# SwiGLU feed-forward on one core: the first 256 rows of x by a crossbar copy instead of TensorE transposes

## The chip, the core and the metric

The kernel runs on one core of a Trainium2 chip. The engines are TensorE (PE in the profile, its weight loads PEld), VectorE (DVE), ScalarE (ACT), GpSimd (POOL) and SyncE (SP). SP and ACT also issue the DMAs, each on a queue of its own; the profile calls these rows SPq and ACTq. The metric is the device time of one execution in microseconds (us), lower is better.

## The reference

x is 1 x 2048 x 640, w_gate and w_up are 640 x 1536, w_down is 1536 x 640, all bf16.

```
def reference(x, w_gate, w_up, w_down):
    g = silu(x @ w_gate)
    u = x @ w_up
    return (g * u) @ w_down
```

## The kernel before

TensorE multiplies over the partition axis, 128 at a time, so x is needed with its 640 columns on partitions: `xT`, 128 partitions x 5 blocks (`KD`) x 2048 rows. The weights lie in on-chip memory as `wg_sb`, `wu_sb` (5 blocks x 1536 columns) and `wd_sb` (12 blocks x 640 columns).

The 2048 rows are taken in four blocks (`sb`) of 512. In each block, for each of 12 column groups (`fc`) of 128, five matmuls of 512 columns make the gate projection `pg` and five the up projection `pu` in PSUM (line 193). ACT takes silu of `pg` into `sg` (line 214), DVE multiplies it by `pu` into `aT` (line 215). When the 12 groups are done, 12 matmuls with `wd_sb` as weights (line 261) make the last 128 output columns, and 4 x 12 matmuls (line 291) the first 512. The last four rows of x go another way: DVE computes their projections as row dot products (line 147) beside TensorE's work. The end of the program cuts the last rows' output into narrow pieces.

The first block begins in another order, in `head()`. TensorE first runs `N_WARM` = 18 matmuls on a tile of ones (`warm`, line 176), which wait only for DVE's memset of that tile (line 109). The first 256 rows of x then arrive as two plain loads of 128 rows (`x_sb`, line 86), one on SP and one on ACT. TensorE transposes them against an identity matrix, which GpSimd makes: five transposes of 128 x 128 for each of the two (`transpose_chunk`, line 185), two into one PSUM tile and three into another. ACT and DVE copy them to `xT` (line 190).

The gate projections of the first four column groups (`EARLY` = 4) follow, held in four PSUM tiles at once. They go block by block over `KD` and in halves of the 512 rows: first rows 0 to 255 for all five blocks, then rows 256 to 511. For block 0 the first half is cut again, into 128 rows and 128 rows. Thus 44 matmuls: 8 of 128 columns and 36 of 256. The four up projections come behind them, 20 matmuls of 512 columns, and from there the regular order.

The weights of the early gate projections, `wg_sb` columns 0 to 511, come as five loads of 128 KB, one for each `kd` (line 115), on SP except for `kd` = 1 on ACT. Behind them, SP's queue holds, in program order: the crossbar copy of x rows 256 to 511 (`turn_x`, line 105; a DMA that transposes on its way), the up weights of groups 0 and 1 and of groups 2 and 3 (line 83), the gate and up weights of groups 4 to 7 and of groups 8 to 11, `wd_sb`, the crossbar copy of rows 512 to 1023, and the loads for the four last rows. ACT, behind its two loads, loads its activation table and runs one silu on a column of ones (line 119), so that the table is there.

`keep_order` writes the issue order of TensorE, ACT, DVE and SP out by hand as the program has it. Waits are placed by the framework from the data that an instruction uses.

Of the kernel before, what the change touches and what calls it, by code (L numbers as in the profile page):

```python
# [7 lines left out]


@with_exitstack  # L10
def _body(
# [8 lines left out]
    nc = tc.nc  # L20
    P = nc.NUM_PARTITIONS
    f32 = mybir.dt.float32
    bf16 = mybir.dt.bfloat16
    ACT = mybir.ActivationFunctionType
    ALU = mybir.AluOpType

    B, S0, D = x.shape
    F = w_gate.shape[1]
    S = B * S0
    x2 = x.rearrange("b s d -> (b s) d")  # L30
    out2 = out.rearrange("b s d -> (b s) d")

    KD = D // P
# [4 lines left out]
    HALF = S_BLK // 2  # L38
    DA = 512
    Q = 32  # L40
    N_WARM = 18
    T = 4
    WT_STEP = 4
    ROW_J = 0
    EARLY = 4
# [3 lines left out]
    consts = ctx.enter_context(tc.tile_pool(name="consts", bufs=1))  # L49
    work = ctx.enter_context(tc.tile_pool(name="work", bufs=3))  # L50
    outp = ctx.enter_context(tc.tile_pool(name="outp", bufs=3))
    psum = ctx.enter_context(
        tc.tile_pool(name="psum", bufs=2, space=bass.MemoryType.PSUM)
    )

    ident = consts.tile([P, P], bf16)
    x_sb = consts.tile([P, HALF // P, D], bf16)
    xT = consts.tile([P, KD, S], bf16)
    wg_sb = consts.tile([P, KD, F], bf16)
    wu_sb = consts.tile([P, KD, F], bf16)  # L60
# [7 lines left out]
    row_s = consts.tile([P, KF, T], f32)  # L68
    prod = consts.tile([P, D], f32)

    make_identity(nc, ident[:])

    x_v = x2.rearrange("(c p) d -> p c d", p=P)
    xt_v = x2.rearrange("s (kd p) -> s kd p", p=P)
    wg_v = w_gate.rearrange("(kd p) f -> p kd f", p=P)
    wu_v = w_up.rearrange("(kd p) f -> p kd f", p=P)
# [2 lines left out]
    def wslice(a, b):  # L79
        return slice(a * P, b * P)  # L80

    def load_w(eng, dst, src, a, b):
        eng.dma_start(out=dst[:, :, wslice(a, b)], in_=src[:, :, wslice(a, b)])

    def load_x(eng, c0, c1):
        eng.dma_start(out=x_sb[:, c0:c1, :], in_=x_v[:, c0:c1, :])  # L86

    def issue_order(a, b):
        tc.add_manual_dep(
# [8 lines left out]
    def keep_order(engine):  # L98

        traced = [i for i in nc.cur_bb.bb.instructions if i.engine == engine]  # L100
        for a, b in zip(traced, traced[1:]):
            issue_order(a, b)

    def turn_x(r0, r1):
        nc.sync.dma_start_transpose(out=xT[:, :, r0:r1], in_=xt_v[r0:r1])

    ones = consts.tile([P, P], bf16)
    silu_first = consts.tile([P, 1], f32)
    nc.vector.memset(ones[:], 1.0)  # L109

    load_x(nc.sync, 0, 1)
    load_x(nc.scalar, 1, 2)
    for kd in range(KD):
        eng = nc.scalar if kd == 1 else nc.sync
        eng.dma_start(
            out=wg_sb[:, kd, wslice(0, EARLY)], in_=wg_v[:, kd, wslice(0, EARLY)]
        )
    turn_x(HALF, S_BLK)
    nc.scalar.activation(silu_first[:], ones[:, 0:1], ACT.Silu)  # L119
    for a in range(0, EARLY, 2):  # L120
        load_w(nc.sync, wu_sb, wu_v, a, a + 2)
    for a, b in W_CHUNKS:
# [6 lines left out]
    def turn_w(dst, src, f0, f1):  # L129
# [7 lines left out]
        out=x_row[:],  # L137
        in_=x2[S - T : S, :].rearrange("t d -> (t d)").partition_broadcast(P),
# [35 lines left out]
    def warm(n):  # L174
        for _ in range(n):
            nc.tensor.matmul(  # L176
                pw[:, 0:P], lhsT=ones[:], rhs=ones[:], start=True, stop=True
            )

    def transpose_chunk(c, parts):  # L180
        c_sl = slice(c * P, (c + 1) * P)
        for copy, tag, k0, k1 in parts:
            pt = psum.tile([P, k1 - k0, P], bf16, tag=tag, name="pt")
            for kd in range(k0, k1):
                nc.tensor.transpose(  # L185
                    out=pt[:, kd - k0, :],
                    in_=x_sb[:, c, kd * P : (kd + 1) * P],
                    identity=ident[:],
                )
            copy(out=xT[:, k0:k1, c_sl], in_=pt[:])  # L190

    def proj_step(ps, w_sb, fc, sb, c0, c1, kd):
        nc.tensor.matmul(  # L193
            ps[:, c0:c1],
            lhsT=w_sb[:, kd, fc * P : (fc + 1) * P],
            rhs=xT[:, kd, sb * S_BLK + c0 : sb * S_BLK + c1],
            start=(kd == 0 and c0 in (0, HALF)),
            stop=(kd == KD - 1),
        )

    def proj(ps, w_sb, fc, sb, c0, c1):
        for kd in range(KD):
            proj_step(ps, w_sb, fc, sb, c0, c1, kd)
# [6 lines left out]
    def gate(pg, pu, sb, fc, n_s):  # L210

        s0 = sb * S_BLK
        sg = work.tile([P, S_BLK], f32, name="sg")
        nc.scalar.activation(sg[:, 0:n_s], pg[:, 0:n_s], ACT.Silu)  # L214
        nc.vector.tensor_tensor(  # L215
            out=aT[:, fc, s0 : s0 + n_s], in0=sg[:, 0:n_s], in1=pu[:, 0:n_s], op=ALU.mult
        )

    def head():
        dve, act = nc.vector.tensor_copy, nc.scalar.copy  # L220
        split = [(act, "po_a", 0, 2), (dve, "po_b", 2, KD)]
        pgs = [
            psum.tile([P, S_BLK], f32, tag="gu", name="pg", bufs=4)
            for _ in range(EARLY)
        ]
        warm(N_WARM)
        for c in range(HALF // P):
            transpose_chunk(c, split)

        steps = [(0, 0, P), (0, P, HALF)]  # L230
        steps += [(kd, 0, HALF) for kd in range(1, KD)]
        steps += [(kd, HALF, S_BLK) for kd in range(KD)]
        for kd, c0, c1 in steps:
            for fc in range(EARLY):
                proj_step(pgs[fc], wg_sb, fc, 0, c0, c1, kd)

        for fc in range(EARLY):
            pu = psum.tile([P, S_BLK], f32, tag=("po_a", "po_b")[fc % 2], name="pu")
            proj(pu, wu_sb, fc, 0, 0, S_BLK)
            gate(pgs[fc], pu, 0, fc, S_BLK)  # L240
        keep_order(mybir.EngineType.PE)
        keep_order(mybir.EngineType.Activation)

    head()
    for sb in range(NSB):
        n_s = S_BLK if sb < NSB - 1 else S_BLK - T
# [26 lines left out]
        for q in range(P // Q):  # L273
            nc.scalar.dma_start(
                out=out2[
                    sb * S_BLK : sb * S_BLK + n_t, DA + q * Q : DA + (q + 1) * Q
                ].rearrange("(i r) c -> r i c", r=Q),
                in_=ot_q[q * Q : (q + 1) * Q, :].rearrange("r (i c) -> r i c", c=Q),
            )

        for j in range(SUB):
# [6 lines left out]
            for c0, c1, tag in cols:  # L288
# [14 lines left out]
                eng = nc.sync if c1 < D else nc.scalar  # L303
# [82 lines left out]
def kernel(tc, *args):  # L386
    _body(tc, *args)
    tc.close()
    tc.compile()
    _trim(tc.nc)  # L390
# [30 lines left out]
```

## Time and profile before

| | |
|---|---|
| median of 3 runs | 163.57 us |
| lowest and highest | 163.18, 163.78 us |
| span of the profiled execution, first to last instruction | 161.8 us |
| TensorE busy in the span | 159.4 us (99%), 808 matmuls |
| VectorE, ScalarE busy | 111.0 us (69%), 42.6 us (26%) |
| first gate matmul, first up matmul | 3.71, 8.79 us |
| moved by DMA | 15.86 MB |

The device time of the profiled execution itself is not recorded beside its span; the median of the runs is 1.8 us above the span. Times in the profile count from the first instruction of the span. A row of the timeline has its start, its length, the engine, the line in the kernel, the operation with output and inputs, and how many instructions are merged in it; in brackets stands how long the engine was idle ahead of it and what ended that. A matmul's length is longer than the distance to the next one, because matmuls are pipelined: the pace is read from the distances of the starts. A stretch row has the stretch, its length, the busy time of PE, PEld, DVE, ACT and POOL with their instructions, the granted clock of TensorE, the share of time in which the DMA engines were busy, and GB/s.

### The profile page before, as it was taken

The numbers are of one execution on the slowest core, as the hardware profiler recorded it, in microseconds if no ns is written. First come the engines' busy times: TensorE is split into PE (matmuls) and PEld (weight loads), VectorE is DVE, ScalarE is ACT, GpSimd is POOL, SyncE is SP. The second block draws the span as 40 slices with busy tenths as digits, with TensorE's granted clock in tenths as the row PEclk, the third lists the DMA queues.
The fourth block names the chain that finished last, engine by engine and source line by source line (L and its number), as shares of the span: only waits on it lengthen the run. The fifth ranks groups of instructions, "written<-read, shape, count | busy, mean of one in ns | idle before, by whom it ended". The sixth has DMA issues, their size and how long they took to land.

```text
span 161.8 us, 2142 instructions
## 1 busy us (share of the span) xinstructions
PE 159.4 (99%) x808; PEld 77.6 (48%) x808; DVE 111.0 (69%) x250; ACT 42.6 (26%) x74; POOL 0.6 (0%) x6
## 2 busy tenths in 40 slices
PE   8999999999999999999999999999999999999995
PEld 7854444444444444444444444444444444445454
DVE  2034223599569999989919999979964999993001
ACT  5051222112222222211222322221214222222121
POOL 1000000000000000000000000000000000000000
PEclk9999999999999999999999999999999999999999
DMA  6999999934189999003110000000321000000312
GB/s 212 231 351 349 361 248 231 222 75 91 34 192 159 235 236 184 4 0 34 65 65 0 0 4 2 0 0 3 62 67 34 0 0 0 0 0 4 48 41 73
DMA packets 41961, 15.86 MB, mean 98 GB/s; under 512 B 33504, under 2 KB 41824, under 8 KB 41952
## 3 DMA queue, kind: packets, MB, share of 16 engines
q1 hardware_dynamic: 33584, 14.93, 37.0%
q10 hardware_dynamic: 8368, 0.80, 3.5%
q8 instruction: 6, 0.10, 0.3%
q14 instruction: 3, 0.02, 0.1%
HBM read 6.88 MB, written 2.62 MB: 59 GB/s over the span
## 4 chain that ended last, share of the span: by engine, by line
PE 97%; DMA 2%; SPq 0%; DVE 0%; issue 0%
PE pg L193 32%; PE pu L193 32%; PE po_a L291 26%; PE po_t L261 6%; DMA wg_sb<-in_w_gate_dram 2%; SPq L86 0%; DVE ot_b L302 0%
## 5 line engine op out<-in xcount | busy, mean ns | idle before, releaser
L193 PE MATMUL pg<-xT,wg_sb 128*128 128x512 bf16 (+3 forms) x264 | 59.8, 363 | 0.1
L193 PE MATMUL pu<-xT,wu_sb 128*128 128x512 bf16 (+1 forms) x240 | 59.1, 379 | 0.0
L215 DVE TENSOR_TENSOR aT<-sg,pu 128x512 bf16<-128x512 f32 (+1 forms) x48 | 32.7, 682 | 32.3 <-PE pu L193 32.3
L214 ACT ACTIVATE sg<-pg 128x512 f32<-128x512 f32 (+1 forms) x48 | 28.4, 597 | 71.2 <-PE pg L193 67.4
L291 PE MATMUL po_a<-wd_sb,aT 128*128 128x512 bf16 (+4 forms) x228 | 42.8, 348 | 0.0
L147 DVE SCALAR_TENSOR_TENSOR prod<-wgT,x_row 128x640 f32<-128x640 bf16 x48 | 39.4, 821 | 1.5 <-DMA wgT<-in_w_gate_dram 0.4
L147 DVE SCALAR_TENSOR_TENSOR prod<-wuT,x_row 128x640 f32<-128x640 bf16 x48 | 39.4, 821 | 1.0
L193 PEld LDWEIGHTS <-wg_sb 128*128 128x128 bf16 x264 | 25.9, 100 | 26.8 <-DMA wg_sb<-in_w_gate_dram 0.4
L193 PEld LDWEIGHTS <-wu_sb 128*128 128x128 bf16 x240 | 23.4, 98 | 28.1 <-DMA wu_sb<-in_w_up_dram 0.3
L291 PEld LDWEIGHTS <-aT 128*128 128x128 bf16 x228 | 20.8, 98 | 21.7
L300 ACT CAST ot<-po_a 128x512 bf16<-128x512 f32 (+2 forms) x17 | 9.5, 559 | 31.8 <-PE po_a L291 20.2
L261 PE MATMUL po_t<-aT,wd_sb 128*128 128x512 bf16 (+1 forms) x48 | 10.4, 366 | 0.0
L261 PEld LDWEIGHTS <-wd_sb 128*128 128x128 bf16 x48 | 4.7, 98 | 5.1
L302 DVE CAST ot_b<-po_a 128x96 bf16<-128x96 f32 (+1 forms) x2 | 0.5, 240 | 9.7 <-PE po_a L291 9.6
L270 ACT CAST ot_t<-po_t 128x512 bf16<-128x512 f32 (+1 forms) x4 | 2.2, 559 | 11.6 <-PE po_t L261 11.6
L147 DVE DVE_READ_ACCUMULATOR prod<-wgT,x_row 128x1 f32 x48 | 3.9, 82 | 0.0
L147 DVE DVE_READ_ACCUMULATOR prod<-wuT,x_row 128x1 f32 x48 | 3.9, 82 | 0.0
L272 DVE STREAM_TRANSPOSE ot_q<-ot_t 128x512 bf16<-128x512 bf16 (+1 forms) x4 | 2.7, 676 | 1.7 <-ACT ot_t L270 1.7
L190 DVE COPY xT<-pt 128x384 bf16<-128x384 bf16 x2 | 0.7, 358 | 2.9 <-PE pt L185 2.9
L176 PE MATMUL pw<-ones 128*128 128x128 bf16 x18 | 2.1, 313 | 0.4 <-DVE ones L109 0.4
L176 PEld LDWEIGHTS <-ones 128*128 128x128 bf16 x18 | 1.8, 147 | 0.4 <-DVE ones L109 0.4
L119 ACT ACT_TABLE_LOAD x1 | 1.3, 1283 | 1.0 <-issue 1.0
(13 smaller groups left out, 4.7 us busy)
## 6 DMA issues: line engine op xcount, KB each, us to landing
wd_sb<-in_w_down_dram SPq DMA_DIRECT2D x1, 1920.0 KB, 13.0
out_dram<-ot SPq DMA_DIRECT2D x15, 128.0 KB, 1.7
wg_sb<-in_w_gate_dram SPq DMA_DIRECT2D x2, 640.0 KB, 7.9
wu_sb<-in_w_up_dram SPq DMA_DIRECT2D x2, 640.0 KB, 8.6
wu_sb<-in_w_up_dram SPq DMA_DIRECT2D x2, 320.0 KB, 4.7
x_row<-in_x_dram SPq DMA_DIRECT2D x1, 640.0 KB, 5.1
wg_sb<-in_w_gate_dram SPq DMA_DIRECT2D x4, 128.0 KB, 3.4
out_dram<-ot_q ACTq DMA_DIRECT2D x12, 32.0 KB, 1.9
```

The lines of the kernel that those rows point to most:

```text
L119: nc.scalar.activation(silu_first[:], ones[:, 0:1], ACT.Silu)
L147: nc.vector.scalar_tensor_tensor(out=prod[:], in0=wT[:, fc, :], scalar=1.0, in1=x_row[:, t, :], op0=ALU.mult, op1=ALU.mult, accum_out=acc[ ...
L176: nc.tensor.matmul(pw[:, 0:P], lhsT=ones[:], rhs=ones[:], start=True, stop=True)
L190: copy(out=xT[:, k0:k1, c_sl], in_=pt[:])
L193: nc.tensor.matmul(ps[:, c0:c1], lhsT=w_sb[:, kd, fc * P : (fc + 1) * P], rhs=xT[:, kd, sb * S_BLK + c0 : sb * S_BLK + c1], start=(kd == 0 ...
L214: nc.scalar.activation(sg[:, 0:n_s], pg[:, 0:n_s], ACT.Silu)
L215: nc.vector.tensor_tensor(out=aT[:, fc, s0 : s0 + n_s], in0=sg[:, 0:n_s], in1=pu[:, 0:n_s], op=ALU.mult)
L261: nc.tensor.matmul(po_t[:], lhsT=wd_sb[:, kf, DA:D], rhs=aT[:, kf, sb * S_BLK : sb * S_BLK + n_t], start=(kf == 0), stop=(kf == KF - 1),)
L270: nc.scalar.copy(ot_t[:], po_t[:])
L272: nc.vector.transpose(out=ot_q[:], in_=ot_t[:])
L291: nc.tensor.matmul(po[:], lhsT=aT[:, kf, s0 : s0 + P], rhs=wd_sb[:, kf, c0:c1], start=(kf == 0), stop=(kf == KF - 1),)
L300: nc.scalar.copy(ot[:], po[:])
```

## The change

The identity, `x_sb`, the two plain loads, the transposes on TensorE and the copies out of PSUM are taken out. Rows 0 to 255 of x come by one crossbar copy straight into `xT`, the first DMA on SP's queue. The first activation (with its table load) now stands ahead of ACT's two loads. Those two are the gate slices of `kd` 0 and 1; slices 2, 3 and 4 come as one load of 384 KB on SP, behind the crossbar copy. The second crossbar copy and all later loads follow in the order they had. The warm-up has 26 matmuls instead of 18. The first half of block 0 is no longer cut in two, so the early gate phase has 40 matmuls of 256 columns. TensorE has 802 matmuls and transposes in all, instead of 808.

```
-    N_WARM = 18
+    N_WARM = 26
...
-    ident = consts.tile([P, P], bf16)
-    x_sb = consts.tile([P, HALF // P, D], bf16)
...
-    make_identity(nc, ident[:])
...
-    load_x(nc.sync, 0, 1)
-    load_x(nc.scalar, 1, 2)
-    for kd in range(KD):
-        eng = nc.scalar if kd == 1 else nc.sync
+    def load_d(eng, k0, k1):
         eng.dma_start(
-            out=wg_sb[:, kd, wslice(0, EARLY)], in_=wg_v[:, kd, wslice(0, EARLY)]
-        )
+            out=wg_sb[:, k0:k1, wslice(0, EARLY)], in_=wg_v[:, k0:k1, wslice(0, EARLY)]
+        )
+
+    turn_x(0, HALF)
+    nc.scalar.activation(silu_first[:], ones[:, 0:1], ACT.Silu)
+    load_d(nc.scalar, 0, 1)
+    load_d(nc.scalar, 1, 2)
+    load_d(nc.sync, 2, KD)
     turn_x(HALF, S_BLK)
-    nc.scalar.activation(silu_first[:], ones[:, 0:1], ACT.Silu)
     for a in range(0, EARLY, 2):
         load_w(nc.sync, wu_sb, wu_v, a, a + 2)
...
-    def transpose_chunk(c, parts):
-        c_sl = slice(c * P, (c + 1) * P)
-        for copy, tag, k0, k1 in parts:
-            pt = psum.tile([P, k1 - k0, P], bf16, tag=tag, name="pt")
-            for kd in range(k0, k1):
-                nc.tensor.transpose(
-                    out=pt[:, kd - k0, :],
-                    in_=x_sb[:, c, kd * P : (kd + 1) * P],
-                    identity=ident[:],
-                )
-            copy(out=xT[:, k0:k1, c_sl], in_=pt[:])
...
         warm(N_WARM)
-        for c in range(HALF // P):
-            transpose_chunk(c, split)
-
-        steps = [(0, 0, P), (0, P, HALF)]
-        steps += [(kd, 0, HALF) for kd in range(1, KD)]
+        steps = [(kd, 0, HALF) for kd in range(KD)]
         steps += [(kd, HALF, S_BLK) for kd in range(KD)]
```

More of the change, by code (lines that the diff above doesn't have):

```diff
@@ L6 @@
 from concourse._compat import with_exitstack
-from concourse.masks import make_identity
 @with_exitstack
@@ L69, in _body @@
     prod = consts.tile([P, D], f32)
-    make_identity(nc, ident[:])
-    x_v = x2.rearrange("(c p) d -> p c d", p=P)
     xt_v = x2.rearrange("s (kd p) -> s kd p", p=P)
@@ L83, in load_w @@
         eng.dma_start(out=dst[:, :, wslice(a, b)], in_=src[:, :, wslice(a, b)])
-    def load_x(eng, c0, c1):
-        eng.dma_start(out=x_sb[:, c0:c1, :], in_=x_v[:, c0:c1, :])
     def issue_order(a, b):
@@ L219, in head @@
     def head():
-        dve, act = nc.vector.tensor_copy, nc.scalar.copy
-        split = [(act, "po_a", 0, 2), (dve, "po_b", 2, KD)]
         pgs = [
```

## The prediction

> **What bounds the kernel now.** I read the page first: engines' busy shares, then the chain that ended last.
>
> ```profile
> span 161.8 us, 2142 instructions
> ...
> PE 159.4 (99%) x808; PEld 77.6 (48%) x808; DVE 111.0 (69%) x250; ACT 42.6 (26%) x74; POOL 0.6 (0%) x6
> ...
> PE 97%; DMA 2%; SPq 0%; DVE 0%; issue 0%
> ```
>
> TensorE is busy 99% of the span, and the chain is TensorE but for 2% of DMA. The change touches only the head, so the next view is the chain in order of time.
>
> ```profile
> 0.45 3.21 DMA wg_sb<-in_w_gate_dram
> 3.71 5.21 PE pg L193 x44
> 8.92 4.37 PE pu L193 x20
> ...
> 148.85 11.10 PE po_a L291 x84
> ```
>
> A gate slice is issued at 0.45 and lands at 3.66; from 3.71 TensorE runs to the end. What happens before the first up matmul is therefore worth its own length, and everything behind it (20 up matmuls, then the rest) is unchanged. I compare one number: when the first up matmul starts. The timeline of the first 15 us gives it, and what stands in front of it.
>
> ```profile
> 0.00 0.39 SPq L86 DMA_DIRECT2D x_sb<-in_x_dram  x1
> 0.13 0.38 ACTq L86 DMA_DIRECT2D x_sb<-in_x_dram  x1
> ...
> 0.39 2.10 PE L176 MATMUL pw<-ones 128*128 128x128 bf16 x18 [0.39 <-DVE ones L109]
> 0.45 1.84 SPq L115 DMA_DIRECT2D wg_sb<-in_w_gate_dram  x4
> 0.54 0.45 ACTq L115 DMA_DIRECT2D wg_sb<-in_w_gate_dram  x1
> ...
> 1.02 1.28 ACT L119 ACT_TABLE_LOAD   x1 [1.02 <-issue]
> 2.31 1.25 PE L185 MATMUL pt<-ident,x_sb 128*128 128x128 bf16 x10
> 2.32 0.20 ACT L119 ACTIVATE silu_first<-ones 128x1 f32<-128x1 bf16 x1
> 2.33 1.91 SPq L105 DMA_TRANSPOSE xT<-in_x_dram  x1
> ...
> 3.60 0.36 DVE L190 COPY xT<-pt 128x384 bf16<-128x384 bf16 x1 [0.17 <-PE pt L185]
> 3.71 4.93 PEld L193 LDWEIGHTS <-wg_sb 128*128 128x128 bf16 x44 [0.41 <-DMA wg_sb<-in_w_gate_dram]
> 3.71 5.21 PE L193 MATMUL pg<-xT,wg_sb 128*128 128x128 bf16 x44
> ...
> 4.29 1.15 SPq L83 DMA_DIRECT2D wu_sb<-in_w_up_dram  x2
> ...
> 8.79 4.49 PE L193 MATMUL pu<-xT,wu_sb 128*128 128x512 bf16 x20
> ...
> 14.06 0.89 PEld L193 LDWEIGHTS <-wu_sb 128*128 128x128 bf16 x5 [0.19 <-DMA wu_sb<-in_w_up_dram]
> 14.20 1.24 PE L193 MATMUL pu<-xT,wu_sb 128*128 128x512 bf16 x5
> ```
>
> The 44 gate matmuls stand between 3.71 and 8.79, 5.08 us. At 14.06 the weight load waits 0.19 for the next up slice: that slice lands with at most 0.14 to spare before its matmul at 14.20. So the stream of loads is nearly as late as TensorE, and an earlier head alone gains little.
>
> How fast those 44 run is in narrow windows of TensorE's timeline (start, length, then the group that starts there), with one row of busy time by stretch.
>
> ```profile
> 4.54 0.59 PE L193 MATMUL pg<-xT,wg_sb 128*128 128x256 bf16 x2
> 4.75 0.59 PE L193 MATMUL pg<-xT,wg_sb 128*128 128x256 bf16 x3
> 4.96 0.49 PE L193 MATMUL pg<-xT,wg_sb 128*128 128x256 bf16 x3
> 5.07 0.38 PE L193 MATMUL pg<-xT,wg_sb 128*128 128x256 bf16 x2
> 6.38 0.46 PE L193 MATMUL pg<-xT,wg_sb 128*128 128x256 bf16 x2
> 6.57 0.27 PE L193 MATMUL pg<-xT,wg_sb 128*128 128x256 bf16 x1
> ```
> ```profile
> 4.50:5.00 0.50, 0.50 (x6) 0.38 (x4) 0.00 (x0) 0.00 (x0) 0.00 (x0) 1.00 1.13 210
> ```
>
> Starts of the same 256-column matmul are 0.21 apart up to 4.96 and 0.11 apart behind it: TensorE runs at half pace until 4.96 and at full pace from there. The granted clock (the 1.00 in the last row) does not show this; the spacing does. Warm-up matmuls (18 from 0.39 to 2.31, 0.107 each) are at the slow pace too. The step of 0.19 at 6.57 is a wait of 0.08 for the second half of x.
>
> **The change part by part.** The SP and ACT queues of the head are rewritten, so these rows of the DMA view (size, us from issue to landing) and of the crossbar copies price it.
>
> ```profile
> wg_sb<-in_w_gate_dram SPq DMA_DIRECT2D x4, 128.0 KB, 3.4
> ...
> x_sb<-in_x_dram SPq DMA_DIRECT2D x1, 160.0 KB, 2.3
> x_sb<-in_x_dram ACTq DMA_DIRECT2D x1, 160.0 KB, 2.6
> wg_sb<-in_w_gate_dram ACTq DMA_DIRECT2D x1, 128.0 KB, 3.3
> ```
> ```profile
> L105 SPq DMA_TRANSPOSE xT<-in_x_dram x1: 1914/1914/1914, 2.3 to 2.3; - x1
> ...
> DMA to landing us min/median/max: 4.2/4.2/4.2
> ```
> ```profile
> L105 SPq DMA_TRANSPOSE xT<-in_x_dram x1: 2732/2732/2732, 44.6 to 44.6; - x1
> ...
> DMA to landing us min/median/max: 5.4/5.4/5.4
> ```
> ```profile
> L83 SPq DMA_DIRECT2D wu_sb<-in_w_up_dram x1: 583/583/583, 4.3 to 4.3; - x1
> ...
> DMA to landing us min/median/max: 4.5/4.5/4.5
> ```
>
> *Removed from TensorE and its neighbours.* The identity (POOL), 10 transposes, 2 ACT and 2 DVE copies go. On the path they cost almost nothing: the last transpose ends at 3.56 and the last copy at 3.96, while the first matmul is released by the gate slice at 3.66. The first eight matmuls, 128 columns each, become four of 256: at the slow pace 8 x 0.107 = 0.86 against 4 x 0.213 = 0.85, nothing; at full pace 4 x 0.109 = 0.44. So the gate phase is 40 matmuls: 40 x 0.109 = 4.36 at full pace.
>
> *x rows 0 to 255.* One crossbar copy at 0.00. A copy of 256 rows among other traffic took 4.2; one of 512 rows on a quieter queue took 2.7 to issue and 5.4 to land. Half that issue (1.4) and the tail behind the issue (4.2 - 1.9 = 2.3 to 5.4 - 2.7 = 2.7) make 3.7 to 4.1, and I take 3.9. Bounds: 2.3 (the plain load of half the rows) and 5.4. A gain is not excluded, since x in TensorE's layout was complete only at 3.96; it needs the slice too.
>
> *Gate slices.* ACT issues the first two behind its table load and the first activation: 0.13 + 1.28 + 0.20 = 1.6, against 0.45 on SP before. Landing 2.6 (ACT's first load) to 3.3 (its second) later: 4.2 to 4.9 for the first slice, some 0.45 more for the second. If ACT's queue goes on while the table loads, the first would land at 0.5 + 2.6 = 3.1. I take 4.2, since little is in flight then. The first matmul starts at the later of 3.9 and 4.2: 4.2, against 3.71. Slices 3 to 5 (384 KB in one load) are issued on SP behind the crossbar copy, at 1.4 to 2.0, and land 3.4 (128 KB) to 4.5 (320 KB) later, 4.8 to 6.5; by size nearer the second, but with a shorter stream ahead: 1.7 + 3.9 = 5.6.
>
> *SP's queue.* Before the up slices SP now issues copy, slices, copy: 1.4 to 1.9, some 0.5, and 1.9, so 3.8 to 4.4, against 4.29. The second crossbar copy is issued at 2.3 instead of 2.33 and lands 4.2 later, 6.5. The first up slice lands 4.5 behind its issue, 8.3 to 8.9. The bytes up to there are the same. Later loads keep their order, so the wait at 14.06 moves with them.
>
> *Warm-up.* 26 x 0.107 = 2.8, so it ends at 3.2 instead of 2.31, still ahead of 4.2: it costs nothing, but TensorE is now idle for 1.0 (3.2 to 4.2); before, the longest pause was 0.33 (2.31 + 10 x 0.107 = 3.38 to 3.71).
>
> *Sum.* Slow pace 4.2 to 4.96: 3.6 matmuls. The eight of slices 1 and 2 are done by 5.4; slices 3 to 5 land at 5.6, which costs 0.2; the other 32 take 32 x 0.109 = 3.5, to 9.1. The second half of x is wanted at 5.6 + 12 x 0.109 = 6.9 and is there; the up slice is there at 8.3 to 8.9. First up matmul at 9.1 against 8.79: 0.3 us later. The span becomes 162.1. The page gives the profiled execution's span alone; the median of the three runs, 163.57, lies 1.8 above it, and I carry that over: 163.57 + 0.3 = 163.9, 0.2% more.
>
> [...] The rows here show full pace at 4.96 with 10 transposes and a pause in the 2.65 us ahead of it. [...]
>
> **The rivals.**
>
> *The pace changes late.* The full pace came 4.57 after the first matmul, over a pause of 0.33. If a pause of 1.0 begins the count again, it comes at 4.2 + 4.57 = 8.8: 21.5 matmuls at 0.213, then 18.5 x 0.109 = 2.0, first up matmul at 10.8, 2.0 later: 165.6. Against it: the warm-up is 8 matmuls longer. From the sum's 9.1, each us of delay costs about 0.5, so slower by more than 0.5% begins at a change near 6.0 (0.3 + 0.5 x 1.0 = 0.8). [...]
>
> *x lands late: a new wait in the place of the old.* If the first crossbar copy needs as long as the 512-row one, 5.4, the 40 matmuls run at full pace from there: 5.4 + 4.36 = 9.8, 1.0 later, 164.6. For it: 256 rows took 1.9 to issue where half of 2.7 would be 1.4, so a part doesn't scale with rows. Against it: the queues are empty.
>
> *Faster.* If ACT's slices go out while the table loads, the copy lands at 3.7, slices 3 to 5 at 4.8 and full pace has come by 3.7 (the longer warm-up), the gate phase ends at 4.8 + 3.5 = 8.3; the up slice at 8.3 allows that: 0.5 earlier, 163.1. Faster by more than 0.5% (0.8) needs the up slices and the one behind the 14.06 wait to be 0.8 earlier as well; only then does it decide, at 162.7 or less.
>
> *The change doesn't do what it says* can't be in the copies, which are gone from the program; "alone" can fail as just said.
>
> **How the numbers follow.** About 0.5%, 0.8 us, is what a measurement of this kernel tells from no change (the runs span 163.18 to 163.78). Forecast, 163.9 with a range of its own from 163.1 to 164.4 (first up matmul between 8.3, the earliest end of the gate phase above, and 9.6): 0.47, which takes in the milder part of the faster case. Late pace, 164.4 to 165.9: 0.26. Late x or late slices, 164.4 to 165.2: 0.17. Faster by more than 0.5%: 0.10. Slower by over 0.5% is the two middle ones, 0.43. For eight in ten the range takes in the forecast, late x and most of the late pace, and the near part of the faster case: 162.8 to 165.6.
>
> **What would show it.** Right: the copy lands near 3.9, the first gate matmul starts near 4.2 released by a gate slice, starts go from 0.21 to 0.11 apart near 5, one short wait for a gate slice near 5.4, the first up matmul near 9.1, and the same work behind it. Wrong: starts still 0.21 apart beyond 6 (late pace); the first gate matmul released by the crossbar copy beyond 4.8 (late x); gate matmuls ending before 8.3 with no wait for an up slice there or at the second group of up matmuls (faster).

## The result: 0.4% slower, and two kinds of runs

| | before | after |
|---|---|---|
| median of 13 runs, us | 163.58 | 164.14 |
| lowest, highest, us | 163.11, 164.23 | 163.59, 165.30 |
| span of the profiled execution, us | 161.8 | 163.7 |

The ratio is 1.0044, with a 95% interval from 1.0027 to 1.0062. The median hides how the runs lie. Six of the 13 are at 163.59 to 163.81, six at 164.68 to 165.30, and one is at 164.14. The kernel before has no such gap. The profiled execution after took 165.03, so it is of the second group. In every run whose span is recorded, of any kernel here, the time is 1.3 above the span (1.26 to 1.39); with the same 1.3 the profiled execution before (161.8) took about 163.1 and was among the quick ones of its kernel.

### The profile page after: what moved, and what is told of

It is laid out like the page before. It is cut to its first block, busy times and chain, and to the rows that moved or that the text cites. A ratio compares the mean times of both kernels' runs of the same rounds, so it can differ in the third digit from the quotient of the medians.

```text
span 163.7 us, 2118 instructions
## 1 busy us (share of the span) xinstructions
PE 160.5 (98%) x802; PEld 78.1 (48%) x802; DVE 110.4 (67%) x248; ACT 42.0 (26%) x72; POOL 0.2 (0%) x4
## 4 chain that ended last, share of the span: by engine, by line
PE 96%; DMA 3%; DVE 0%; issue 0%
PE pg L174 33%; PE pu L174 32%; PE po_a L266 26%; PE po_t L236 6%; DMA xT<-in_x_dram 3%; DVE ot_b L277 0%
## 5 line engine op out<-in xcount | busy, mean ns | idle before, releaser
L174 PE MATMUL pg<-xT,wg_sb 128*128 128x512 bf16 (+2 forms) x260 | 61.2, 374 | 0.9 <-DMA xT<-in_x_dram 0.9
L174 PEld LDWEIGHTS <-wg_sb 128*128 128x128 bf16 x260 | 26.5, 102 | 28.4 <-issue 0.6
L169 PE MATMUL pw<-ones 128*128 128x128 bf16 x26 | 3.0, 313 | 0.4 <-DVE ones L100 0.4
L169 PEld LDWEIGHTS <-ones 128*128 128x128 bf16 x26 | 2.7, 149 | 0.4 <-DVE ones L100 0.4
```

The lines of the kernel that those rows point to most:

```text
L169: nc.tensor.matmul(pw[:, 0:P], lhsT=ones[:], rhs=ones[:], start=True, stop=True)
L174: nc.tensor.matmul(ps[:, c0:c1], lhsT=w_sb[:, kd, fc * P : (fc + 1) * P], rhs=xT[:, kd, sb * S_BLK + c0 : sb * S_BLK + c1], start=(kd == 0 ...
```

## The profile after

The page and the chain in order of time (start, length), of the changed kernel:

```profile
span 163.7 us, 2118 instructions
...
PE 160.5 (98%) x802; PEld 78.1 (48%) x802; DVE 110.4 (67%) x248; ACT 42.0 (26%) x72; POOL 0.2 (0%) x4
...
PE 96%; DMA 3%; DVE 0%; issue 0%
```
```profile
0.00 4.26 DMA xT<-in_x_dram
4.30 6.59 PE pg L174 x40
10.89 4.32 PE pu L174 x20
```

The chain begins with the crossbar copy and not with a gate slice. The gate phase of 40 matmuls takes longer than that of 44 took before (6.59 against 5.21). The timeline of the head shows the steps:

```profile
0.00 1.33 SPq L96 DMA_TRANSPOSE xT<-in_x_dram  x1
0.12 1.28 ACT L108 ACT_TABLE_LOAD   x1
...
0.38 0.96 ACTq L103 DMA_DIRECT2D wg_sb<-in_w_gate_dram  x2
...
0.40 2.96 PE L169 MATMUL pw<-ones 128*128 128x128 bf16 x26 [0.40 <-DVE ones L100]
1.38 0.58 SPq L103 DMA_DIRECT2D wg_sb<-in_w_gate_dram  x1
...
2.01 1.89 SPq L96 DMA_TRANSPOSE xT<-in_x_dram  x1
3.56 0.10 PEld L174 LDWEIGHTS <-wg_sb 128*128 128x128 bf16 x1 [0.48 <-DMA wg_sb<-in_w_gate_dram]
3.95 1.46 SPq L77 DMA_DIRECT2D wu_sb<-in_w_up_dram  x2
4.30 6.59 PE L174 MATMUL pg<-xT,wg_sb 128*128 128x256 bf16 x40 [0.95 <-DMA xT<-in_x_dram]
...
10.73 4.48 PE L174 MATMUL pu<-xT,wu_sb 128*128 128x512 bf16 x20
```

ACT's two loads go out at 0.38, in the middle of its table load (0.12 to 1.40). The first slice is there at 3.5, when its weight load runs (3.56); what TensorE waits for, until 4.30, is x. The first up matmul starts at 10.73, 1.94 behind the 8.79 of before, which is the difference of the two spans. Where those 1.94 lie is seen in narrow windows of TensorE's timeline:

```profile
8.31 0.51 PE L174 MATMUL pg<-xT,wg_sb 128*128 128x256 bf16 x2
8.52 0.52 PE L174 MATMUL pg<-xT,wg_sb 128*128 128x256 bf16 x3
...
8.77 0.38 PE L174 MATMUL pg<-xT,wg_sb 128*128 128x256 bf16 x2
8.87 0.38 PE L174 MATMUL pg<-xT,wg_sb 128*128 128x256 bf16 x2
```

The starts are 0.21 apart up to 8.52 (one at 8.66 lies between) and 0.10 to 0.11 apart behind 8.77. Full pace comes near 8.6, where it came at 4.96 before: half of the gate phase runs at half pace.

The same kernel was run again, and that time the profile fell on a run of the first group (span 162.3, 163.58 us):

```profile
0.40 2.96 PE L169 MATMUL pw<-ones 128*128 128x128 bf16 x26 [0.40 <-DVE ones L100]
...
3.54 0.10 PEld L174 LDWEIGHTS <-wg_sb 128*128 128x128 bf16 x1 [0.46 <-DMA wg_sb<-in_w_gate_dram]
...
4.29 1.10 PE L174 MATMUL pg<-xT,wg_sb 128*128 128x256 bf16 x8 [0.94 <-DMA xT<-in_x_dram]
...
5.77 3.39 PEld L174 LDWEIGHTS <-wg_sb 128*128 128x128 bf16 x32 [0.67 <-DMA wg_sb<-in_w_gate_dram]
5.77 3.67 PE L174 MATMUL pg<-xT,wg_sb 128*128 128x256 bf16 x32 [0.39 <-DMA wg_sb<-in_w_gate_dram]
```

Here the eight matmuls of slices 0 and 1 are at full pace from the first (4.29 to 5.2), and the ninth waits until 5.77 for the load with slices 2 to 4 (the prediction counts from 1 and calls them 3 to 5). The 32 that follow take 32 x 0.109 = 3.5, so the up matmuls start near 9.27 (the trace lacks the record of the first; its weight load is at 9.17). So in these two profiles the bounds differ: in the second group the late pace, in the first the late slices.

## The experiments

All comparisons are with the kernel before, run on the same chip beside it. Theory: the pause of TensorE between the warm-up and the first gate matmul puts off the change of pace in some runs. Rival: the late pace comes with the new loads, or with the transposes that are gone.

**The changed kernel again.** No edit.

> The changed kernel unchanged, beside the kernel before on one chip. If the pause of 1.1 us leaves the change of pace to the moment at which a run falls: again two groups, one at 163.5 to 164.2 and one at 164.6 to 165.3, each with about a third to two thirds of the runs. If the two groups belonged to the chip of the first comparison: one group alone.

Measured: ratio 1.0059 (1.0028 to 1.0091), median 164.26 against 163.56. Six of 12 runs are at 163.58 to 163.89 and six at 164.62 to 165.64. The two groups belong to the kernel, not to one chip.

**The pause filled.**

```
-    N_WARM = 26
+    N_WARM = 36
```

> The changed kernel with 36 warm-up matmuls instead of 26. 10 x 0.107 = 1.07 us more, so the warm-up ends near 4.2, where the first gate matmul (4.30 in the changed kernel) can start. Theory, the pause delays the change to full pace: the runs near 165 vanish, all runs lie like the better half of the changed kernel, 163.5 to 164.0; in the profile the pace changes before 6.9 and the first up matmul starts by 9.9. Rival, the late pace comes with the new loads or with the missing transposes and not with the pause: still about half the runs near 165.

Measured: ratio 1.0020 (1.0007 to 1.0034), 163.62 to 164.15. None of 12 runs is near 165. The timeline and two narrow windows:

```profile
0.40 4.02 PE L169 MATMUL pw<-ones 128*128 128x128 bf16 x36 [0.40 <-DVE ones L100]
...
4.37 5.40 PE L174 MATMUL pg<-xT,wg_sb 128*128 128x256 bf16 x40
...
9.60 0.59 PE L174 MATMUL pu<-xT,wu_sb 128*128 128x512 bf16 x2
```
```profile
5.82 0.57 PE L174 MATMUL pg<-xT,wg_sb 128*128 128x256 bf16 x2
6.03 0.46 PE L174 MATMUL pg<-xT,wg_sb 128*128 128x256 bf16 x2
6.22 0.49 PE L174 MATMUL pg<-xT,wg_sb 128*128 128x256 bf16 x3
6.33 0.49 PE L174 MATMUL pg<-xT,wg_sb 128*128 128x256 bf16 x3
```

The first gate matmul starts nearly where it did (4.37), and full pace comes at 6.2. The loads are those of the changed kernel, so the rival falls: the pause makes the group near 165. Ten more warm-up matmuls take the second group away; 0.2% to the kernel before remains. On another chip the same kernel gave the same:

> The kernel with 36 warm-up matmuls again, beside the next one on one chip: 163.6 to 164.2, median near 163.75, one group.

Measured: ratio 1.0024 (1.0009 to 1.0039), 163.64 to 164.23, one group but for three runs at 164.07 to 164.23. Its profile fell on a run with the full pace already inside the warm-up, and there the bound is again the load with slices 2 to 4:

```profile
5.91 3.67 PE L174 MATMUL pg<-xT,wg_sb 128*128 128x256 bf16 x32 [0.40 <-DMA wg_sb<-in_w_gate_dram]
```

So with the pause filled, the run with an early change of pace (3.6) waits for the slices and the one with a later change (6.2, above) does not; they took 163.72 and 163.91 us.

**The pause lengthened.**

```
-    N_WARM = 26
+    N_WARM = 18
```

> The changed kernel with the 18 warm-up matmuls of the kernel before; the pause grows from about 1.1 to 2.0 us (2.3 to 4.3). Theory: the late pace comes in nearly all runs, median near 165.1. Rival (the pause is not the cause): the same mix as the changed kernel, median near 164.1.

Measured: ratio 1.0095 (1.0064 to 1.0125), six runs from 164.25 to 165.79, median 165.21. The group at 163.6 is gone. Narrow windows of its TensorE timeline put full pace at 8.98:

```profile
8.57 0.57 PE L174 MATMUL pg<-xT,wg_sb 128*128 128x256 bf16 x2
8.79 0.46 PE L174 MATMUL pg<-xT,wg_sb 128*128 128x256 bf16 x2
8.98 0.49 PE L174 MATMUL pg<-xT,wg_sb 128*128 128x256 bf16 x3
9.09 0.49 PE L174 MATMUL pg<-xT,wg_sb 128*128 128x256 bf16 x3
```

So the share of late runs goes with the length of the pause: none of 22 with 36 warm-up matmuls, about half of 25 with 26, and with 18 all six are slower than the first group. The start of the warm-up (0.40) and the landing of x (4.2 to 4.4) are fixed in these runs, so a longer pause is also less work of TensorE ahead of the gate phase; they can't tell the two apart.

**The pause filled with transposes.** Here the question is whether transposes keep TensorE's pace up as matmuls do. Behind the warm-up of the changed kernel:

```
+    ident = consts.tile([P, P], bf16)
+    make_identity(nc, ident[:])
...
         warm(N_WARM)
+        pt = psum.tile([P, 8, P], bf16, tag="po_a", name="pt")
+        for i in range(10):
+            nc.tensor.transpose(out=pt[:, i % 8, :], in_=ones[:], identity=ident[:])
```

> The changed kernel with the identity made on GpSimd again and 10 transposes of the tile of ones on TensorE behind the 26 warm-up matmuls, so that transposes fill the pause up to about 4.2 us; their result is not used. If transposes count as work of TensorE for its pace: like the kernel with 36 warm-up matmuls, all runs 163.5 to 164.2, median near 163.75. [...]

Measured: ratio 1.0026 (1.0016 to 1.0036), 163.66 to 164.22, no run of the second group among 12. Its timeline:

```profile
3.14 1.27 PE L211 MATMUL pt<-ident,ones 128*128 128x128 bf16 x10
...
4.22 5.62 PE L177 MATMUL pg<-xT,wg_sb 128*128 128x256 bf16 x40
```

The transposes fill the pause as well as matmuls do: with ten more of either no run is above 164.23 (12 with transposes, 22 with matmuls), where 12 of 25 with neither are at 164.62 or more. No run has transposes alone.

**A pause in the kernel before.**

```
-    N_WARM = 18
+    N_WARM = 10
```

> The kernel before with 10 warm-up matmuls instead of 18: a pause from 1.46 to 2.31 us ahead of the transposes, loads and transposes untouched. Theory with transposes that count as work of TensorE: a pause of 0.85 like that of the changed kernel, so part of the runs is 1.5 to 1.7 us slower (near 165.2), the others stay near 163.6. [...] Rival (the pause is not the cause): 163.6 in all runs.

Measured: ratio 1.0028 (1.0008 to 1.0048), 163.24 to 164.77, median 163.80. The pause does harm there too, with no change of any load. But the runs lie evenly, and none reaches 165.2: the size I expected of a late run was too large by 0.4 or more, or none of the 12 was fully late. In the profile the transposes ran from 2.43, a pause of about 1.0, and full pace came at 6.8:

```profile
2.43 1.25 PE L185 MATMUL pt<-ident,x_sb 128*128 128x128 bf16 x10 [0.79 <-DMA x_sb<-in_x_dram]
...
6.46 0.54 PE L193 MATMUL pg<-xT,wg_sb 128*128 128x256 bf16 x2
6.67 0.44 PE L193 MATMUL pg<-xT,wg_sb 128*128 128x256 bf16 x2
6.84 0.49 PE L193 MATMUL pg<-xT,wg_sb 128*128 128x256 bf16 x3
6.95 0.38 PE L193 MATMUL pg<-xT,wg_sb 128*128 128x256 bf16 x2
```

If transposes did nothing for the pace, the pause would be 2.0 (1.46, by 10 x 0.107 behind 0.40, to the first gate matmul at 3.47), as long as that of the changed kernel with 18 warm-up matmuls, whose ratio is 1.0095; by that nearly all runs should have been late, and one, at 164.77, comes near.

**The copy really alone.** From the kernel with 36 warm-up matmuls:

```
-    load_d(nc.scalar, 0, 1)
-    load_d(nc.scalar, 1, 2)
+    load_d(nc.sync, 0, 1)
+    load_d(nc.sync, 1, 2)
```

> The kernel with 36 warm-up matmuls, and the two gate slices of ACT issued on SP behind the crossbar copy, so that the copy is really alone (in the changed kernel ACT issued them at 0.38, 1.3 us behind the copy's issue begins its first packet). Theory, the slices' packets slow the copy: it lands by 3.6 instead of 4.3, the first gate matmul then waits for its slice (issued at 1.4, landing near 4.0), first gate matmul at 4.0, time 163.5. Rival, the copy has its own pace: it still lands at 4.1 to 4.3, the slices behind it land no earlier than 4.0, the first gate matmul stays at 4.3 or later, 163.8 to 164.0.

Measured: ratio 1.0059 (1.0043 to 1.0075), median 164.38; with the slices on ACT the ratios were 1.0020 and 1.0024. Landing of the copy and timeline:

```profile
L96 SPq DMA_TRANSPOSE xT<-in_x_dram x1: 1324/1324/1324, 0.0 to 0.0; - x1
...
DMA to landing us min/median/max: 3.4/3.4/3.4
```
```profile
0.40 3.49 PE L169 MATMUL pw<-ones 128*128 128x128 bf16 x36 [0.40 <-DVE ones L100]
1.38 1.52 SPq L103 DMA_DIRECT2D wg_sb<-in_w_gate_dram  x3
...
4.70 1.05 PE L174 MATMUL pg<-xT,wg_sb 128*128 128x256 bf16 x8 [0.81 <-DMA wg_sb<-in_w_gate_dram]
...
6.56 3.67 PE L174 MATMUL pg<-xT,wg_sb 128*128 128x256 bf16 x32 [0.81 <-DMA wg_sb<-in_w_gate_dram]
```

The first half of the theory holds: with no load issued before 1.38, the copy lands at 3.4, where in the other profiles with the copy whole, ACT's two loads beside it, it lands at 4.2 to 4.4. So those loads cost it some 0.9. The second half fails: behind the copy the first slice is there only at 4.70, later than x was, and slices 2 to 4 at 6.56 instead of 5.77. To put everything behind the copy moves the wait from x to the slices.

**The copy in two.** From the changed kernel:

```
-    turn_x(0, HALF)
+    turn_x(0, P)
+    turn_x(P, HALF)
...
-        steps = [(kd, 0, HALF) for kd in range(KD)]
+        steps = [(0, 0, P), (0, P, HALF)]
+        steps += [(kd, 0, HALF) for kd in range(1, KD)]
```

> The changed kernel (26 warm-up matmuls) with rows 0 to 127 and 128 to 255 in two crossbar copies, and the first block of the gate phase cut in two as in the kernel before. If the copy's time goes with its rows beyond a fixed part, the first half lands near 3.4, the first gate matmul starts at 3.5 (slice 0 lands at 3.52), the pause shrinks to 0.4 and the runs near 165 vanish: 163.5 to 163.8. If a fixed part or the slices beside it set the landing, the first half lands at 4.0 or later and the mix of the changed kernel stays.

Measured: ratio 1.0170 (1.0149 to 1.0191), five runs from 165.65 to 166.49, median 166.13. Neither expected time came: none of the five is faster than the slowest run of the changed kernel (165.64).

```profile
0.00 2.60 SPq L96 DMA_TRANSPOSE xT<-in_x_dram  x2
...
3.98 0.58 PE L175 MATMUL pg<-xT,wg_sb 128*128 128x128 bf16 x4 [0.64 <-DMA xT<-in_x_dram]
...
4.77 1.44 PE L175 MATMUL pg<-xT,wg_sb 128*128 128x128 bf16 x8 [0.20 <-DMA xT<-in_x_dram]
...
6.60 3.58 PE L175 MATMUL pg<-xT,wg_sb 128*128 128x256 bf16 x20 [0.40 <-DMA wg_sb<-in_w_gate_dram]
```

Each half copy takes 1.3 to issue, as much as the whole one (1.33): up to 256 rows the time to issue does not go with the rows here. The first half lands at about 3.9, slices 2 to 4 are issued 1.3 later and in use at 6.6, and TensorE pauses three times. Full pace comes at 9.2 in this run (starts at 8.92, 9.14, 9.26). How much of the loss is the pace and how much the later slices isn't shown.

**Only the merged slices, in the kernel before.**

```
-    for kd in range(KD):
-        eng = nc.scalar if kd == 1 else nc.sync
+    for eng, k0, k1 in ((nc.sync, 0, 1), (nc.scalar, 1, 2), (nc.sync, 2, KD)):
         eng.dma_start(
```

(with the slices `k0:k1` inside)

> The kernel before with its gate slices 2 to 4 in one load of 384 KB, as in the changed kernel; x by plain loads and TensorE as before. SP issues the first up slice near 3.5 instead of 4.29, so it lands near 8.0 instead of 8.75 as in the changed kernel (8.0). If the stream of loads held the kernel before: 0.1 to 0.5 us faster, 163.0. If TensorE's slow pace up to 5 us or later held it: no change, within 0.2 us; and if slices 2 to 4 now land too late for the ninth gate matmul, 0.2 to 0.4 us slower.

Measured: ratio 0.9998 (0.9983 to 1.0013), no difference.

```profile
3.48 1.96 SPq L83 DMA_DIRECT2D wu_sb<-in_w_up_dram  x2
...
5.75 3.67 PE L192 MATMUL pg<-xT,wg_sb 128*128 128x256 bf16 x32 [1.11 <-DMA wg_sb<-in_w_gate_dram]
...
9.26 1.03 PE L192 MATMUL pu<-xT,wu_sb 128*128 128x512 bf16 x4
```

The up slices are issued 0.8 earlier (3.48 against 4.29), but the merged load holds the ninth gate matmul until 5.75 in a run with an early pace, as in the first group of the changed kernel (5.77). Its first up matmul is at 9.26, 0.47 behind that of the kernel before, whose profile was also of an early pace (4.96). So here the merged load costs time and the earlier up slices bring none. Why the medians are alike all the same isn't shown.

**The slices apart again, with 36 warm-up matmuls.**

```
-    load_d(nc.sync, 2, KD)
+    for kd in range(2, KD):
+        load_d(nc.sync, kd, kd + 1)
```

> The kernel with 36 warm-up matmuls, slices 2 to 4 in three loads of 128 KB on SP instead of one of 384 KB. If the one large load is what holds the runs with an early change of pace (it lands at 5.73, the ninth gate matmul starts at 5.77): slice 2 lands near 4.9 and slice 4 near 5.7, early runs start the first up matmul near 8.9 instead of 9.3, the lowest time falls by 0.2 to 0.4 and the median by 0.1 to 0.3. Against it: two more issues on SP (some 0.8 us) put the first up slice from 8.0 to 8.8 and the next crossbar copy later, so the gain is given back: no change or 0.1 to 0.3 slower.

Measured: ratio 1.0038 (1.0023 to 1.0052), five runs from 163.68 to 164.14, median 164.08. The gain did not come, though slice 2 landed at 5.1 (issued at 1.4, 3.7 on its way) instead of 5.7 to 5.9. Its profile fell on a run with full pace at 6.4, in which the merged load would not have been waited for either, so whether the early runs gain stays open; the median of the five does not.

**The small pause of the kernel before filled.** Three more matmuls on the tile of ones behind its transposes:

```
         for c in range(HALF // P):
             transpose_chunk(c, split)
+        warm(N_FILL)
```

> The kernel before with 3 warm-up matmuls (0.32 us) between its transposes and its first gate matmul, so that its pause of 0.33 is filled; nothing else. If even a pause of 0.33 delays the change of pace in some runs: its slower runs (163.9 to 164.4, about one in eight) vanish and the median falls by 0.1 to 0.2. If so short a pause is free: no change, or up to 0.1 slower where the fill delays the first gate matmul.

Measured: ratio 1.0007 (0.9981 to 1.0032), 163.03 to 165.33. No change in the median. In the profiled run the gate slice was there only at 3.97 and the first gate matmul at 3.98, so 0.3 of pause was left behind the three matmuls; whether so short a pause matters stays open. One run, 165.33, was slower than any of the kernel before and as slow as the second group, though the profile of this kernel shows no pause near 1 us: the pause need not be the only thing that makes a run slow, and nothing here says what did. No version beat the kernel before.

## Why the prediction held, and where it did not

- **Forecast (163.9, within 0.5%).** The time moved by 0.44%, 0.56 us, against 0.3 forecast. That the median came so near is in part luck: only one of the 13 runs lies between the groups, and it is the median; had one run fallen into the other group, it would be 163.81 or 164.68. The first group has the forecast's times: first gate matmul at 4.29 (4.2 forecast), slices 2 to 4 in use at 5.77 (5.6), first up matmul near 9.27 (9.1), span 162.3 (162.1). It does not have all of its steps: x and not a gate slice released the first gate matmul, the pace was full from that matmul on and not from 4.96, and the wait for slices 2 to 4 was 0.55 (the eighth done at 5.22, by the starts) and not 0.2.
- **The rival of the late pace** is the second group: full pace near 8.6 (8.8 forecast), first up matmul at 10.73 (10.8), 1.94 us later in the span (2.0). The chance of 0.26 was given for the median; of the runs, about half went that way. The step that failed is that the sum left the change of pace at 4.96, where the kernel before had it, and held the longer warm-up against the longer pause. The pause was 1.1 us (warm-up to 3.2, first gate matmul at 4.30; 1.0 forecast), the change came before 4.29 in one profile and near 8.6 in the other, and filling the pause with ten matmuls, or ten transposes, removed the whole group. If transposes did nothing for the pace, the pause before would have been 1.40 (2.31 to 3.71), longer than the new one, and no reason for a later change. No run shows that: with ten of them in the pause all 12 runs are at 163.66 to 164.22.
- **The removed transposes and copies** were put at nothing on the path, because the gate slice released the first matmul. So it was: nothing was gained there, and the gate phase in the first group starts 0.58 later than before.
- **The crossbar copy** was to land at 3.9 and landed at 4.26. The term was too small for a reason the text had named only as a chance: ACT's loads did not queue behind its table load but went out at 0.38, and beside them the copy takes 4.3 instead of 3.4. So the wait was one for x and not for the slice. Of the sum's two terms the issue was right (1.33 against 1.4) and the tail behind it too small: 2.9 (4.26 - 1.33) against 2.3 to 2.7, and 2.1 where no load was beside it. The 1.9 that the other copy of 256 rows took to issue was not the price of its rows either: with three slices ahead of it, it was issued at 2.95 and took 1.32.
- **SP's queue.** The first up slice was issued at 3.95 (3.8 to 4.4 forecast), and no wait for an up slice shows at the first up matmul. The kernel before did have one there, of about 0.04 (its last gate matmul starts at 8.64, 0.11 behind the one at 8.54), which the sum does not name:

```profile
8.79 4.00 PEld L193 LDWEIGHTS <-wu_sb 128*128 128x128 bf16 x20 [0.15 <-DMA wu_sb<-in_w_up_dram]
```

- **The warm-up** ends at 3.2 as forecast. "Costs nothing" was right for its length; the pause behind it was what cost.
- **A delay of 1 us costs 0.5.** Filled with 36 matmuls, the kernel starts its gate phase 0.66 later than before (4.37 against 3.71) and is 0.33 to 0.42 slower in the median. This is near the 0.5, an estimate from the two spacings, for a pace that changes at a time of its own: a matmul missed at 0.213 is made up at 0.109. But it is not a test of it, since in one of the two profiles with 36 matmuls the pace set the time and in the other the slices.
- **The anchor.** I carried the difference of median and span, 1.8, from the profiled execution over to the forecast. The profiled execution had been a quick one, with 1.3 between span and time; the rest of the 1.8 is the spread from run to run, not a constant. With 1.3 the forecast's span of 162.1 is 163.4 (the first group is at 163.59 to 163.81) and that of the late pace, 163.8, is 165.1 (the second is at 164.68 to 165.30).
- **"Faster"** would have needed the copy at 3.7 and slices 2 to 4 at 4.8. ACT's early issue came true, but it is what delays the copy.

## What to carry to other kernels

In this kernel a head that ends in a wait costs not the wait alone but also what the wait does to TensorE's pace (spans of 163.7 and 162.3 with the same wait for x, to 4.30 and 4.29): fill the time up to the measured landing of the first operand with matmuls, and look at the spread of the runs, since a median may stand between two groups. A DMA that is first in program order isn't alone (the copy landed at 4.26 with ACT's loads beside it, at 3.4 without): look at the other queue's issue row, because a table load on ACT held its activation here (until 1.42) and not its loads (0.38). Three loads merged into one took 0.58 to issue instead of 1.51, but put the landing of the first from 5.1 to between 5.7 and 5.9; look whether something waits for the first one.

## What the runs showed of the hardware that was not expected

- Loads issued by ACT went out during its table load (issue at 0.38, table load 0.12 to 1.40).
- A crossbar copy of 128 rows took as long to issue as one of 256 (two in 2.60, one in 1.33), while one of 512 in the kernel before took 2.73.
- Two loads of 128 KB on the other queue put the copy's landing from 3.4 (one profile) to 4.2 to 4.4 (seven).
- The moment at which full pace comes differs between executions, with no change of the program: in the changed kernel once before the first gate matmul at 4.29 and once near 8.6; 36 warm-up matmuls took 4.02 us in one run and 3.49 in the one with the slices behind the copy, where the starts go from 0.107 apart to 0.055 at 3.2, inside the warm-up. In the profiles it lies from 3.2 to 6.4 where no pause ahead of it was longer than 0.4, and, with a pause of some 1 us or more, from before 4.3 to 9.2. No run here shows what sets it.
